# Fused attention and two gated layers: scores of the first batch in one step per buffer, a copy moved to ScalarE, a small sum moved to GpSimd

## The chip, the core and the metric

The kernel runs on one core of a Trainium2 chip. The metric is the time of one execution on the device in microseconds; less is better. The engines named below are TensorE (PE: matmuls, with weight loads PEld beside them), VectorE (DVE), ScalarE (ACT), GpSimd (POOL) and the queue that issues DMAs (SP). Each works through its own queue in the order in which it was written.

## What is computed

Three layers in a row, on a batch of 4 with 576 positions, 8 heads of 64 and 512 channels:

```python
q_rot, k_rot = rotate(q), rotate(k)                  # rotary positions
scores = q_rot @ k_rot.T / 8
attn = exp(scores - max(scores)); attn /= sum(attn) + 1e-9
x = attn @ v                                         # heads side by side: 512 channels
xk, xr = mix of x and x one position earlier
k = relu(xk @ w_k); v = k * k @ w_v
x = sigmoid(xr @ w_r) * v
h = relu(x @ w_in); u, v = halves of h
out = (u * (w_spatial @ normalized(v) + b_spatial)) @ w_out
```

## The kernel before, in words

Attention works in 72 **units**, 18 for each of the 4 batches. A batch has 4 pairs of heads; a pair's 576 query rows make four units of 128 rows and a rest of 64, and the rests of two neighbouring pairs share a unit, the **tail** (units 4 and 13 of a batch). In a common unit the two buffers (`j` = 0 and 1) are the two heads of the pair: head 0 lies in partitions 0 to 63, head 1 in 64 to 127, so their score matmuls use different row groups of TensorE. In a tail the two buffers are the two pairs.

The steps of a unit, by their names in `unit(m)`:

- `scores` (line 338 in the first batch, in plain fp32; lines 327 and 330 later, with split operands): rotated q against rotated k into two score buffers `s` in PSUM, of two banks each, one set for all units. So a unit's scores wait until the exponentials of the unit before have read these buffers.
- `top(j)` (342): VectorE takes the negative maximum of each row of buffer j. `expo(j)` (347): ScalarE's exponential, with the row sums, into `p`.
- `total` (351): the sums plus 1e-9, two numbers per row, on ScalarE. `norm` (354): VectorE's reciprocal. `spread` (358): ScalarE spreads the result over 64 columns.
- `turn(n)`, n = 0, 1, 2 (lines 367 to 381): TensorE turns P through PSUM in three parts; part 0 needs the first exponential, part 1 the second, part 2 holds what is left of P and the spread reciprocals. `take(n)` (395) copies them to `pt`: parts 0 and 1, 128x512, on ScalarE, part 2, 128x256, on VectorE (in a tail each part is two smaller copies).
- After every second common unit (once in nine units, after the tail that follows it) `values` (402) multiplies `pt` by v, twenty matmul records, and `gather` (414) scales the result.

Beside this run the rotation of q and k for later pairs (`prep`, lines 249 to 272, VectorE mostly), the splitting of 16 blocks of the weights `w_k` and `w_v` into a high and a low part (lines 151 to 174, on ScalarE, VectorE and GpSimd), and, from the second batch on, the next layer's matmuls for the batch that is finished (`feed`, lines 498 and 537). During the first batch no such matmuls are there to fill TensorE.

The order of all this is written out before the kernel is built by a planner (`Plan`). Every step is added with an engine, an assumed duration, the steps it needs, and a rank. The planner plays the steps through: at each point it takes, of an engine's steps that are ready within 0.3 us (on TensorE at once), the one of lowest rank, and so it fixes each engine's queue. GpSimd's steps and some of VectorE's are assumed to exclude each other. The assumed durations thus decide places in the queues, while the times on the chip may be others.

Of the kernel before, what the change touches and what calls it, by code (L numbers as in the profile page):

```python
# [7 lines left out]
F32 = mybir.dt.float32  # L8
# [3 lines left out]
AF = mybir.ActivationFunctionType  # L12
ALU = mybir.AluOpType
AX = mybir.AxisListType
PSUM = bass.MemoryType.PSUM
# [10 lines left out]
EXACT = NP  # L26
WB, GB, WB2, GB2 = 3, 2, 3, 2
RAW, ROT, VB, PFB, PTB, XTS = 2, 4, 2, 3, 2, 6
KB, RLB, VSB = 4, 2, 1
EARLY, EVERY = 24, 2.9  # L30
WAIT, SWITCH, BONUS = 0.3, 0.1, 0.0
SIDES = slice(0, HALF), slice(HALF, S)
HEAD = slice(0, 64), slice(64, 128)
# [17 lines left out]
class Plan:  # L51
# [5 lines left out]
    def add(self, eng, us, fn, deps=(), rank=0.0, after=0.12, take=None, give=None, port=False, kind=None):  # L57
        s = Step(eng, us, fn, deps, rank, after, take, give, port, kind)
        self.steps.append(s)
        return s  # L60
# [44 lines left out]
def body(ctx: ExitStack, tc, qp, kp, vp, cs, mu_k, mu_r, w_k, w_v, w_r, w_in, w_sp, b_sp, w_out, out):  # L105
    nc = tc.nc

    const = ctx.enter_context(tc.tile_pool(name="const", bufs=1))
# [6 lines left out]
    ps_m = ph1p.enter_context(tc.tile_pool(name="ps_m", bufs=1, space=PSUM))  # L115
    att = ExitStack()
    at = att.enter_context(tc.tile_pool(name="att", bufs=1, side="right"))
    ps_s = att.enter_context(tc.tile_pool(name="ps_s", bufs=2, space=PSUM, side="right"))
    ps_t = att.enter_context(tc.tile_pool(name="ps_t", bufs=1, space=PSUM, side="right"))
    stage = [at, WB, GB]  # L120

# [5 lines left out]
    ends = [[at.tile([128, 128], F32R, tag=f"qe{i}{k}", name=f"qe{i}{k}") for k in range(2)] for i in range(2)]  # L127
    ident = const.tile([128, 128], F32, name="ident")
    mix4 = const.tile([128, NP, 4], F32, name="mix4")
    epsc = const.tile([128, 3], F32, name="epsc")  # L130
    warm = const.tile([128, 1], F32, name="warm")

    turn_of = {"ww": 0, "wg": 0}
# [72 lines left out]
    add = plan.add  # L206
# [5 lines left out]
    ropes, vloads, exps, turned, valued, xdone, stored = {}, {}, {}, {}, {}, {}, {}  # L212
# [5 lines left out]
    def constants():  # L218
        nc.gpsimd.memset(epsc[:, 0:1], 1e-6)
        nc.gpsimd.memset(epsc[:, 1:2], -0.5)  # L220
        nc.gpsimd.memset(epsc[:, 2:3], 1e-9)
        nc.gpsimd.memset(ident, 0.0)
        for x in ends[0] + ends[1]:
            nc.gpsimd.memset(raw(x), 0.0)
        nc.gpsimd.affine_select(out=ident, in_=ident, compare_op=ALU.not_equal, fill=1.0, base=0,
                                pattern=[[-1, 128]], channel_multiplier=1)
# [76 lines left out]
    units, scored, duos, freed = {}, {}, {}, {}  # L303

    def unit(m):
        w = which(m)
        tail = len(w) == 2
        st = units[m] = {}
# [3 lines left out]
                for n in ((4 * g + 1, 4 * g + 2) if tail else (4 * g + (k - (k > 4)) // 2,))]  # L312
        duo = into[0]

        def scores(halves=(0, 1)):
            if 0 in halves:
                st["s"] = [ps_s.tile([128, 2, 512], F32, tag="s", name=f"s{2 * m + j}") for j in range(2)]
                st["sm"] = at.tile([128, 4, 2], F32, tag="sm", bufs=4, name=f"sm{m}")
            ps = st["s"]
            if w[0][0] >= EXACT:  # L320
                for u, (i, c) in enumerate(w):
                    t = qk[i]
                    for n, (a, b) in enumerate((("hi", "hi"), ("hi", "lo"), ("lo", "hi"))):
                        for h in range(2):
                            x, f = slice(h * HALF, h * HALF + HALF), dict(start=n == 0, stop=n == 2)
                            if tail:
                                nc.tensor.matmul(ps[u][:, h, :HALF], ends[i % 2][a == "lo"], t[b, 1][:, x], **f)  # L327
                            else:
                                for j, r in enumerate(HEAD):
                                    nc.tensor.matmul(ps[j][:, h, :HALF], t[a, 0][r, 128 * c:128 * c + 128], t[b, 1][r, x], **f)  # L330
                return
            for u, (i, c) in enumerate(w):
                q, k = qk[i][0], qk[i][1]
                for h in halves:
                    for j in range(2):
                        r = HEAD[j]
                        o = ps[u][r, h, :HALF] if tail else ps[j][:, h, :HALF]
                        nc.tensor.matmul(o, q[r, 128 * c:min(128 * c + 128, S)], k[r, h * HALF:(h + 1) * HALF],  # L338
                                         start=True, stop=True)

        def top(j):
            nc.vector.tensor_reduce(st["sm"][:, 0, j:j + 1], st["s"][j][:, :, :HALF], axis=AX.XY, op=ALU.max, negate=True)  # L342
# [5 lines left out]
                                 bias=st["sm"][:, 0, j:j + 1], scale=1.0, accum_out=st["sm"][:, 1, j:j + 1])  # L348

        def total():  # L350
            nc.scalar.activation(st["sm"][:, 2, :], st["sm"][:, 1, :], AF.Identity, bias=epsc[:, 2:3])

        def norm():
            nc.vector.reciprocal(st["sm"][:, 3, :], st["sm"][:, 2, :])
# [28 lines left out]
        def take(n, eng):  # L383
            for u, d in enumerate(into):
                if "pt" not in d:
                    d["pt"] = at.tile([128, 10, 320], F32, tag=f"pt{d['n'] % PTB}", name=f"pt{d['n']}")
                o = d["pt"][:, 4 * n:min(4 * n + 4, 10), 256:320]
                if not tail:
                    o, x = d["pt"][:, 4 * n:min(4 * n + 4, 10), 128 * part:128 * part + 128], st["t", n]
                    x = x if n < 2 else x[:, 0:2, :]  # L390
                elif n < 2:
                    x = st["t", n].rearrange("p c (h q) -> p (c h) q", h=2)[:, 4 * u:4 * u + 4, :]
                else:
                    x = st["t", n][:, u, :].rearrange("p (h q) -> p h q", h=2)
                nc.scalar.copy(o, x) if eng == "ACT" else nc.vector.tensor_copy(o, x)  # L395
# [24 lines left out]
        need = [ropes[i] for i, _ in w]  # L420
        if m == 0:
            need = ropes["first"][1] + [add("PE", 0.6, lambda: scores((0,)), ropes["first"][0], -1.0, kind="s")]
        scored[m] = s = add("PE", 0.55 if m == 0 else (2.0 if tail else 1.07) if w[0][0] < EXACT else 1.58 if tail else 0.8, (lambda: scores((1,))) if m == 0 else scores, need + [exps.get((m - 1, j)) for j in range(2)], m - 1.0, kind="s")
        mx = [add("DVE", 0.75, lambda j=j: top(j), [s], m - 0.6) for j in range(2)]
        for j in range(2):
            exps[m, j] = add("ACT", 0.93, lambda j=j: expo(j), [mx[j]] + [turned.get((m - PFB, n)) for n in range(4)],
                             m - 0.5)
        t = add("ACT", 0.2, total, [exps[m, 1]], m - 0.3)
        nm = add("DVE", 0.17, norm, [t], m - 0.3)
        sp = add("ACT", 0.26, spread, [nm], m - 0.3)  # L430
        ready = [[exps[m, 0], exps[m, 1]] if tail else [exps[m, 0]], [exps[m, 1]], [sp]]
        for n in range(3):
            turned[m, n] = add("PE", (0.5, 0.5, 0.8)[n] if tail else (0.44, 0.44, 0.22)[n], lambda slot, n=n: turn(n, slot),
                               ready[n], m + 0.1 * n, take="t", kind="t")
            eng = ("ACT", "ACT", "DVE")[n]
            x = add(eng, ((0.68, 0.68, 0.55) if tail else (0.59, 0.59, 0.42))[n], lambda n=n, eng=eng: take(n, eng),
                    [turned[m, n]] + [y for d in into for y in freed.get(d["n"] - PTB, [])], m - 0.2, give=turned[m, n])
            for d in into:
                d["ev"].append(x)
        if part and k != 3 or tail:  # L440
# [3 lines left out]
            x = add("DVE", 0.49 if duo["cols"] > 256 else 0.42, gather, [v] + mixed.get(i - XTS, []), m + 0.5, give=v)  # L444
# [449 lines left out]
```

## Time and profile before

| what | value |
|---|---|
| median of 3 runs | 777.69 us (777.66 to 781.87) |
| the profiled execution | 777.82 us |
| its span, first to last instruction | 776.0 us |
| TensorE busy (share of the span) | 740.8 us (95%) |
| VectorE | 481.0 us (62%) |
| ScalarE | 463.6 us (60%) |
| GpSimd | 112.2 us (14%) |
| chain that ended last | TensorE 88%, VectorE 4%, ScalarE 3%, DMA 3% |

The profile lists instructions with their start, their duration, and, where an engine stood idle before one, what released it. Busy shares over the whole span mix stages: attention runs to about 450 us, the other layers after it, and the first batch is over at about 102 us. So the rows below are of stretches.

### The profile page before, as it was taken

Reading aid. Unit: us, or ns where it says so; the run is one execution under the profiler, and the core shown is the slowest. Engines: PE = TensorE matmul, PEld = TensorE weight load, DVE = VectorE, ACT = ScalarE, POOL = GpSimd, SP = SyncE. Lnnn points to the kernel's source line nnn. Section 1 sums busy time; section 2 is a strip of 40 time slices with the busy share of each in tenths; the row PEclk is TensorE's granted clock in tenths of the full one; section 3 lists DMA queues with packets and bytes.
Section 4 is the critical chain, followed back from the end, with each engine's and each line's share of the span. In section 5 each row is a group of like instructions: output and inputs, shape, how many; then the busy total and the mean of one; then the engine's idle time right before and its main releaser. Section 6 shows DMA issues by size and latency. Waiting matters only on the chain.

```text
span 776.0 us, 14283 instructions
## 1 busy us (share of the span) xinstructions
PE 740.8 (95%) x5696; PEld 649.9 (84%) x5696; DVE 481.0 (62%) x881; ACT 463.6 (60%) x1061; POOL 112.2 (14%) x132
## 2 busy tenths in 40 slices
PE   4788889999999999999999999999999999999997
PEld 2555569788888888888888898989989999998997
DVE  5988898888777877687856434246463342545111
ACT  3878898778777878778777644245333322533221
POOL 1432424011211211211111000002020000101000
PEclk9999999999999999999999999999999999999999
DMA  8363540542342442533232175072201212010101
GB/s 294 116 201 122 175 129 20 164 149 99 134 163 85 141 156 88 182 113 126 92 131 70 51 268 210 24 264 57 87 1 62 63 46 77 17 31 1 62 1 62
DMA packets 35268, 84.13 MB, mean 108 GB/s; under 512 B 4545, under 2 KB 10433, under 8 KB 35202
## 3 DMA queue, kind: packets, MB, share of 16 engines
q1 hardware_dynamic: 34658, 82.63, 31.6%
q8 instruction: 45, 0.74, 0.4%
q10 hardware_dynamic: 544, 0.59, 0.3%
q14 instruction: 21, 0.17, 0.1%
HBM read 60.65 MB, written 22.55 MB: 107 GB/s over the span
## 4 chain that ended last, share of the span: by engine, by line
PE 88%; DVE 4%; ACT 3%; DMA 3%; issue 0%; SPq 0%; ACTq 0%
PE mv L537 13%; PE mk L498 11%; PE v L402 11%; PE t L378 9%; PE sp L673 8%; PE r L673 7%; PE u L673 7%; PE hv L737 6%; PE o L673 6%; PE s L330 6%; PE s L338 3%; ACT pf L347 1%; DVE raw L249 1%; DMA wi<-wd 1%; PE s L327 1%; DVE sm L342 1%
## 5 line engine op out<-in xcount | busy, mean ns | idle before, releaser
L342 DVE TENSOR_REDUCE sm<-s 128x1 f32<-128x576 f32 x144 | 107.2, 751 | 36.9 <-PE s L330 30.5
L347 ACT ACTIVATE pf<-s,sm 128x576 f32<-128x576 f32 x144 | 107.0, 745 | 14.1 <-DVE sm L342 13.0
L537 PE MATMUL mv<-kh,wv 128*128 128x288 f32 x512 | 114.1, 305 | 1.2 <-ACT kh L512 1.2
L498 PE MATMUL mk<-x,wk 128*128 128x288 f32 x768 | 110.2, 298 | 0.4 <-ACT rl L505 0.4
L395 ACT COPY pt<-t 128x512 f32<-128x512 f32 (+1 forms) x160 | 84.8, 542 | 34.3 <-PE t L378 32.0
L498 PEld LDWEIGHTS mk<-x,wk 128*128 128x128 f32 x768 | 102.9, 188 | 0.7 <-ACT rl L505 0.6
L378 PE MATMUL t<-ident,pf 128*128 128x128 f32 x512 | 82.5, 284 | 14.0 <-ACT pf L347 14.0
L537 PEld LDWEIGHTS mv<-kh,wv 128*128 128x128 f32 x512 | 85.6, 191 | 5.4 <-issue 3.9
L378 PEld LDWEIGHTS t<-ident,pf 128*128 128x128 f32 x512 | 56.6, 141 | 39.9 <-issue 16.4
L402 PE MATMUL v<-pt,vt 128*64 128x256 f32 (+1 forms) x640 | 87.5, 411 | 0.0
L537 PE MATMUL mv<-kl,wv 128*128 128x288 f32 x256 | 76.5, 299 | 0.6 <-DVE kl L516 0.6
L402 PEld LDWEIGHTS v<-pt,vt 128*64 128x64 f32 x640 | 44.3, 136 | 31.7 <-issue 4.1
L673 PE MATMUL sp<-ws,vn 128*128 128x288 f32 x384 | 53.9, 295 | 0.0
L673 PE MATMUL r<-xr,wr 128*128 128x288 f32 x384 | 52.5, 296 | 1.2 <-ACT vs L543 1.2
L673 PE MATMUL o<-g,wo 128*128 128x288 f32 x384 | 52.9, 296 | 0.5 <-ACT os L796 0.5
L673 PEld LDWEIGHTS r<-xr,wr 128*128 128x128 f32 x384 | 51.7, 188 | 1.8 <-ACT vs L543 1.5
L673 PEld LDWEIGHTS sp<-ws,vn 128*128 128x128 f32 x384 | 52.4, 188 | 0.7
L673 PEld LDWEIGHTS o<-g,wo 128*128 128x128 f32 x384 | 51.7, 188 | 1.4 <-ACT os L796 1.2
L673 PE MATMUL u<-x,wi 128*128 128x288 f32 x384 | 52.0, 296 | 0.0
L673 PEld LDWEIGHTS u<-x,wi 128*128 128x128 f32 x384 | 51.6, 188 | 0.3
L537 PEld LDWEIGHTS mv<-kl,wv 128*128 128x128 f32 x256 | 48.9, 191 | 1.2 <-DVE kl L516 1.2
L249 DVE TENSOR_TENSOR raw<-raw,cst 128x1152 f32<-128x1152 f32 (+1 forms) x34 | 45.6, 1344 | 5.7 <-DMA raw<-kp 4.9
(347 smaller groups left out, 1200.3 us busy)
## 6 DMA issues: line engine op xcount, KB each, us to landing
raw<-kp SPq DMA_DIRECT2D x15, 576.0 KB, 3.8
raw<-qp SPq DMA_DIRECT2D x15, 576.0 KB, 4.3
vt<-vp SPq DMA_DIRECT2D x16, 320.0 KB, 3.8
xd<-xt SPq DMA_DIRECT2D x16, 288.5 KB, 3.2
vd<-vs SPq DMA_DIRECT2D x32, 144.0 KB, 1.8
v<-vd SPq DMA_DIRECT2D x16, 288.0 KB, 2.7
out<-os SPq DMA_DIRECT2D x15, 288.0 KB, 2.1
wi<-wd SPq DMA_DIRECT2D x8, 512.0 KB, 9.1
```

Of the source, the lines that this page charges most:

```text
L249: nc.vector.tensor_tensor(t["raw", k][:, :, z], t["raw", k][:, :, z], cst[:, :, z], op=ALU.mult)
L330: nc.tensor.matmul(ps[j][:, h, :HALF], t[a, 0][r, 128 * c:128 * c + 128], t[b, 1][r, x], **f)
L338: nc.tensor.matmul(o, q[r, 128 * c:min(128 * c + 128, S)], k[r, h * HALF:(h + 1) * HALF], start=True, stop=True)
L342: nc.vector.tensor_reduce(st["sm"][:, 0, j:j + 1], st["s"][j][:, :, :HALF], axis=AX.XY, op=ALU.max, negate=True)
L347: nc.scalar.activation(st["p"][:, j, :].rearrange("p (a b) -> p a b", a=2), st["s"][j][:, :, :HALF], AF.Exp, bias=st["sm"][:, 0, j:j + 1], ...
L378: nc.tensor.transpose(pt[:, c, :], p[:, n, k:k + 128], ident)
L395: nc.scalar.copy(o, x) if eng == "ACT" else nc.vector.tensor_copy(o, x)
L402: nc.tensor.matmul(pv[HEAD[j], z], v[:, 4 * j + c if c < 4 else 8 + j, :], pt[:, 4 * j + c if c < 4 else 8, z], start=c == 0, stop=c == 4)
L498: nc.tensor.matmul(ps[:, :HALF], wk[w][:, c, fc * 128:(fc + 1) * 128], a[:, c, :], start=k == 0, stop=k == 11)
L537: nc.tensor.matmul(xs["v", dc][:, :HALF], wv[w][:, fc, dc * 128:(dc + 1) * 128], a, start=k == 0, stop=k == 23)
L673: nc.tensor.matmul(ps[:, h, :HALF], w, a[:, h * HALF:(h + 1) * HALF], start=m == 0, stop=m == n - 1)
L737: nc.tensor.matmul(ps[:, :FS], x[a][:, d, c:c + 128], wi[w][:, d, FS:], start=k == 0, stop=k == 11)
```

## The change

Four things, all for units of the first batch (m < 18):

- `scores` takes a list of buffers. For units 1 to 17 the planner gets two steps, one for each buffer, instead of one for both: step j needs the exponential j of the unit before (not both), the second step needs the first, and `top(j)` needs only step j. In a common unit the matmuls of head 0 are thus written before those of head 1, where before the two heads alternated. The assumed duration is 0.95 us for each step; it was 1.07 us for both (2.0 in a tail). The score buffers get a tag of their own each, with one buffer per tag instead of two buffers of one tag.
- `total` is an addition of two columns on GpSimd, with an assumed 0.37 us, instead of ScalarE's activation. For later units it stays on ScalarE, but its assumed duration is 0.3 instead of 0.2 us. The constants get a fourth column.
- `take(2)` is on ScalarE instead of VectorE, with an assumed 0.38 us (0.55 in a tail).
- Unit 0 keeps its scores in two steps of half the keys each.

```diff
-    ps_s = att.enter_context(tc.tile_pool(name="ps_s", bufs=2, space=PSUM, side="right"))
+    ps_s = att.enter_context(tc.tile_pool(name="ps_s", bufs=1, space=PSUM, side="right"))
...
-        def scores(halves=(0, 1)):
-            if 0 in halves:
-                st["s"] = [ps_s.tile([128, 2, 512], F32, tag="s", name=f"s{2 * m + j}") for j in range(2)]
+        def scores(halves=(0, 1), buffers=(0, 1)):
+            if 0 in halves and 0 in buffers:
+                st["s"] = [ps_s.tile([128, 2, 512], F32, tag=f"s{j}", name=f"s{2 * m + j}") for j in range(2)]
...
                 q, k = qk[i][0], qk[i][1]
+                if tail and u not in buffers:
+                    continue
                 for h in halves:
-                    for j in range(2):
+                    for j in range(2) if tail else buffers:
...
         def total():
-            nc.scalar.activation(st["sm"][:, 2, :], st["sm"][:, 1, :], AF.Identity, bias=epsc[:, 2:3])
+            if m < 18:
+                nc.gpsimd.tensor_tensor(st["sm"][:, 2, :], st["sm"][:, 1, :], epsc[:, 2:4], op=ALU.add)
+            else:
+                nc.scalar.activation(st["sm"][:, 2, :], st["sm"][:, 1, :], AF.Identity, bias=epsc[:, 2:3])
...
-        scored[m] = s = add("PE", 0.55 if m == 0 else (2.0 if tail else 1.07) if w[0][0] < EXACT else 1.58 if tail else 0.8, (lambda: scores((1,))) if m == 0 else scores, need + [exps.get((m - 1, j)) for j in range(2)], m - 1.0, kind="s")
-        mx = [add("DVE", 0.75, lambda j=j: top(j), [s], m - 0.6) for j in range(2)]
+        before = [exps.get((m - 1, j)) for j in range(2)]
+        if 0 < m < APART:
+            sc = [add("PE", 0.95, lambda j=j: scores(buffers=(j,)), need + [before[j]], m - 1.0 + 0.05 * j, kind="s") for j in range(2)]
+            sc[1].deps.append(sc[0])
+        else:
+            sc = [add("PE", 0.55 if m == 0 else (2.0 if tail else 1.07) if w[0][0] < EXACT else 1.58 if tail else 0.8,
+                      (lambda: scores((1,))) if m == 0 else scores, need + before, m - 1.0, kind="s")] * 2
+        scored[m] = sc[1]
+        mx = [add("DVE", 0.75, lambda j=j: top(j), [sc[j]], m - 0.6) for j in range(2)]
...
-        t = add("ACT", 0.2, total, [exps[m, 1]], m - 0.3)
+        t = add(*(("POOL", 0.37) if m < 18 else ("ACT", 0.3)), total, [exps[m, 1]], m - 0.3)
...
-            eng = ("ACT", "ACT", "DVE")[n]
-            x = add(eng, ((0.68, 0.68, 0.55) if tail else (0.59, 0.59, 0.42))[n], lambda n=n, eng=eng: take(n, eng),
+            eng = "ACT" if m < 18 else ("ACT", "ACT", "DVE")[n]
+            x = add(eng, ((0.68, 0.68, 0.55) if tail else (0.59, 0.59, 0.38 if eng == "ACT" else 0.42))[n], lambda n=n, eng=eng: take(n, eng),
```

## Rows read from the trace of the kernel before

**Rows 1.** Busy time by stretch: stretch, its length, PE, PEld, DVE, ACT, POOL (instructions), clock, DMA.

```profile
12.00:102.00 90.00, 73.99 (x528) 46.88 (x528) 79.06 (x145) 74.12 (x184) 32.00 (x26) 1.00 0.48 158
20.00:40.00 20.00, 15.50 (x128) 10.00 (x128) 19.08 (x35) 16.51 (x43) 7.95 (x7) 1.00 0.35 118
140.00:450.00 310.00, 310.00 (x2648) 265.85 (x2647) 231.73 (x434) 237.75 (x594) 46.01 (x42) 1.00 0.36 120
```

**Rows 2.** ScalarE in order of time: start, duration, engine, line, operation, tiles, shape.

```profile
17.06 0.75 ACT L347 ACTIVATE pf<-s,sm 128x576 f32<-128x576 f32 x1
...
62.56 0.59 ACT L395 COPY pt<-t 128x512 f32<-128x512 f32 x1
63.05 0.75 ACT L347 ACTIVATE pf<-s,sm 128x576 f32<-128x576 f32 x1
...
66.65 0.59 ACT L395 COPY pt<-t 128x512 f32<-128x512 f32 x1 [0.32 <-PE t L378]
67.13 0.75 ACT L347 ACTIVATE pf<-s,sm 128x576 f32<-128x576 f32 x1
...
72.52 0.75 ACT L347 ACTIVATE pf<-s,sm 128x576 f32<-128x576 f32 x1
...
102.40 0.75 ACT L347 ACTIVATE pf<-s,sm 128x576 f32<-128x576 f32 x1
```

**Rows 3.** TensorE in order of time, units 9 to 11; the last two: narrower windows.

```profile
60.11 0.66 PE L378 MATMUL t<-ident,pf 128*128 128x128 f32 x4
60.70 1.24 PE L338 MATMUL s<-rot,rot 64*128 64x288 f32 x8
61.87 0.66 PE L378 MATMUL t<-ident,pf 128*128 128x128 f32 x4
...
63.94 0.66 PE L378 MATMUL t<-ident,pf 128*128 128x128 f32 x4 [1.19 <-ACT pf L347]
64.52 1.50 PE L338 MATMUL s<-rot,rot 64*128 64x288 f32 x8
...
66.76 2.90 PE L402 MATMUL v<-pt,vt 128*64 128x256 f32 x20
69.59 0.66 PE L378 MATMUL t<-ident,pf 128*128 128x128 f32 x4
...
61.05 0.65 PE L338 MATMUL s<-rot,rot 64*128 64x288 f32 x4
61.29 0.65 PE L338 MATMUL s<-rot,rot 64*128 64x288 f32 x4
```

**Rows 4.** The chain that ended last: start, duration, what.

```profile
114.16 2.31 PE v L402 x20
```

**Rows 5.** VectorE in order of time, the same units.

```profile
61.97 0.76 DVE L342 TENSOR_REDUCE sm<-s 128x1 f32<-128x576 f32 x1 [0.20 <-PE s L338]
62.78 0.42 DVE L395 COPY pt<-t 128x256 f32<-128x256 f32 x1
63.12 0.75 DVE L342 TENSOR_REDUCE sm<-s 128x1 f32<-128x576 f32 x1
...
65.80 0.76 DVE L342 TENSOR_REDUCE sm<-s 128x1 f32<-128x576 f32 x1 [0.32 <-PE s L338]
```

**Rows 6.** Line 395 by stretch (DVE, ACT); groups by shape: busy us, mean ns.

```profile
12.00:102.00 90.00, 7.30 (x19) 20.51 (x40) 1.00 0.48 158
...
L395 ACT COPY pt<-t 128x256 f32<-128x256 f32 x8 | 2.5, 376 | 0.0
L351 ACT ACTIVATE sm<-sm,epsc 128x2 f32<-128x2 f32 x18 | 5.3, 296 | 0.6
...
L744 POOL TENSOR_TENSOR st<-st,epsc 128x1 f32<-128x1 f32 x18 | 5.6, 316 | 200.1 <-DVE st L743 200.1
```

**Rows 7.** TensorE in order of time at the end of a tail's first part.

```profile
34.35 0.51 PE L338 MATMUL s<-rot,rot 64*128 64x288 f32 x1
34.41 0.22 PE L367 MATMUL t<-ident,pf 64*128 64x64 f32 x1
34.47 1.19 PE L338 MATMUL s<-rot,rot 64*128 64x288 f32 x7
```

More of the change, by code (lines that the diff above doesn't have):

```diff
@@ L30 @@
 EARLY, EVERY = 24, 2.9
+APART = 18
 WAIT, SWITCH, BONUS = 0.3, 0.1, 0.0
@@ L129, in body @@
     mix4 = const.tile([128, NP, 4], F32, name="mix4")
-    epsc = const.tile([128, 3], F32, name="epsc")
+    epsc = const.tile([128, 4], F32, name="epsc")
     warm = const.tile([128, 1], F32, name="warm")
@@ L220, in constants @@
         nc.gpsimd.memset(epsc[:, 1:2], -0.5)
-        nc.gpsimd.memset(epsc[:, 2:3], 1e-9)
+        nc.gpsimd.memset(epsc[:, 2:4], 1e-9)
         nc.gpsimd.memset(ident, 0.0)
```

## Prediction

> **What bounds the kernel now.** I read the busy time by stretch first. In the long middle, 140 to 450 us, TensorE is busy 310.00 of 310 us: that stretch costs what its matmuls cost, and no step of the other engines' queues shortens it [rows 1]. The first batch, 12 to 102 us, is different: TensorE 73.99 of 90 us, VectorE 79.06, ScalarE 74.12, GpSimd 32.00. No engine is full there, so it is waits that are to be looked for, and what is saved in it moves the start of the full stretch and so the end.
>
> The next view is ScalarE in order of time. The first exponential of unit 1 starts at 17.06 us, that of unit 18 at 102.40: 85.34 us for 17 units, 5.02 us each [rows 2]. From unit 10 (63.05) to unit 12 (72.52) two units take 9.47 us; this pair recurs, tails apart, and I work with it.
>
> In the same pair TensorE runs: turning of the last unit's first part (60.11), scores (60.70), turning of the other parts (61.87), then a wait; again first part (63.94), scores (64.52), other parts, values (66.76), up to the next first part at 69.59 [rows 3]. Three waits lie in these 9.48 us. (1) 1.19 us before 63.94, for the exponential. (2) 0.26 us inside the second scores block, 1.50 against 1.24 us: its second buffer was still being read. (3) 0.59 us inside the values, 2.90 against 2.31 us of the same twenty matmuls where nothing is late [rows 3, 4]: they wait for ScalarE's copy of the second part, which ends at 66.65 + 0.59 = 67.24, after they began at 66.76 [rows 2, 3]. Sum 2.04 us in 9.48; over 17 units, 8.5 pairs, 17.3 us.
>
> What ends last in wait 1? The maximum of the first buffer is done at 61.97 + 0.76 = 62.73, but its exponential starts at 63.05, because ScalarE first does the copy of 62.56 that stands ahead of it in its queue [rows 2, 5]. In the next unit the maximum is done at 65.80 + 0.76 = 66.56 and the exponential starts at 67.13, behind the copy of 66.65: 0.57 us late. And the second maximum stands behind VectorE's copy of the last part: 61.97 to 63.12 is 1.15 us for a 0.76 us instruction.
>
> **The change part by part.**
> *VectorE's copies go.* Between 12 and 102 us that is 19 copies, 7.30 us of the 79.06 [rows 6]; the next instruction starts 0.34 us after such a copy (62.78 to 63.12 [rows 5]), so the queue gets 19 x 0.34, some 6 us, back. What is late next is the second exponential, which then waits for the first one (745 ns) and not for VectorE.
>
> *ScalarE gets them and loses the sum.* A 128x256 copy on ScalarE shows 376 ns in the tail units [rows 6]; between nothing and the 0.59 us of a 128x512 copy [rows 2] I take that for all 20 pieces (16 units with one, two tails with two smaller ones). 20 x 0.376 = 7.5 us in, 18 x 0.296 = 5.3 us out [rows 6]: ScalarE rises by 2.2 us to some 76 of 90. It hides as long as ScalarE has those idle 14 us; without that cover it would be 2.2 us. Behind the moved copy wait the next exponentials and the values, which need it last of their five steps, some 1.8 us after they start.
>
> *GpSimd gets the sum.* Its queue holds the weights' additions, 26 instructions in 32.00 us, 1.2 us each [rows 1]. A tiny addition there takes 316 ns [rows 6], about the 296 ns that ScalarE took, so the chain sum, reciprocal, spread, third part only gains a hop. Busy 36% of the time, GpSimd makes a sum wait half an instruction, 0.6 us, in one unit of three, or longer where the addition ahead itself waits; VectorE's reciprocal waits with it, and the maxima behind that in VectorE's queue. Bounds: 0, if the planner's place for it fits, to 18 x 0.36 x 0.6 = 4 us. I take 0.5 us: the reciprocal has time, since the third part is turned after the second. The memset of one more column is nothing: it runs before the first scores.
>
> *Scores in two steps.* One block now alternates the two heads (row groups), eight matmul records in 1.17 us to the next start (60.70 to 61.87). In two steps all four records of one head come before those of the other. The price per unit: 0, if the second head's records overtake and run beside the first's; four pair steps more, 4 x 0.24 = 0.96 us, if they queue (pairs start at 61.05 and 61.29 [rows 3]); a second block's 1.17 us if work is put between the two. The row nearest to this: a record of the next scores starts at 34.35, before the last turning record of the step ahead of it in the queue, at 34.41 [rows 7]. Matmuls of one row group do start ahead of older ones of the other. So I take 0.1 us per unit, 15 units (the two tails already went buffer by buffer, unit 0 keeps its own two steps): 1.5 us, lying in wait 1. For this the Trainium skill has a contrary rule ("TensorE: Matmul & The Clock Gate", Part 3): matmuls start and end strictly in program order, only weight loads are pulled ahead. By it the two heads would queue, and this step of the sum would be 15 x 0.96 us instead of 1.5; the row at 34.35 disagrees. The chance for it stands with the rivals.
>
> *What the two steps give.* The first buffer's scores need only the first exponential. Placed by that, their maximum, and then the exponential, is due sooner in the written-out order, and stands ahead of the copy of the second part instead of behind it. That is worth 0.32 us in the one unit and 0.57 in the other, 0.89 us per pair at most; the values then get their copy later, so wait 3 is not won but moved, unless the next scores are put before them. Of wait 2 nothing is gained as long as the first part's turning (0.59 us) fills it. I take a bit over half of 0.89, 0.5 us per pair, plus 0.2 for the second maximum no longer behind a copy: 0.7 x 8.5 = 6.0 us.
>
> *The written-out order after unit 18.* The planner's cost of the sum on ScalarE goes from 0.2 to 0.3, so later steps may change places. I cost this at nothing: TensorE's full queue hides it [rows 1]; if it opened gaps, each would cost its own length.
>
> Sum: -6.0 + 0.5 + 1.5 = -4.0 us. The profiled execution took 777.82 us around a span of 776.0; the median of the runs is 777.69, 0.13 less. **773.8 us** on the profiled one, so 773.7 as a median.
>
> **The rivals.**
> *Packed queues (faster).* If the two buffers decouple wholly, the fullest engine sets the pace. ScalarE then has 76 us of work where it needs 90, VectorE 72. VectorE reaches 19.08 of 20 us today where it is fullest [rows 1], 95%; ScalarE at 95% needs 80 us: 10 us less, 768. For it: all three waits are of order, not of work. Against: TensorE's values (2.3 us or more) still stand between scores in one queue, and 95% on every engine is rare.
>
> *Unpaired scores (slower).* If the second head's records do queue behind the first's, TensorE gets 15 x 0.96 = 14.4 us. Wait 1, 1.19 x 8.5 = 10.1 us, can take that up; the other 4.3 us lengthen the batch: 782. If the planner also puts other work between the steps, 15 x 1.17 - 10.1 = 7.4 us, 785. It decides from 10.1 / 15 = 0.67 us more per unit. For it: the alternation of heads is what keeps a block at 1.17 us. Against: the overtaking record [rows 7]. The rule of the Trainium skill named above is this rival's.
>
> *It doesn't do what it says (no change).* The first part's turning and the first scores step come due together, after the same exponential. If the turning stays ahead, the first scores start where they do now, 0.59 us after it; the written-out order shifts little, GpSimd's late sums take back 2 to 4 us, and the time is 776 to 779, taken at 777.5.
>
> **How the numbers follow.** Chances: forecast 0.42 (own range 770 to 776), packed 0.17, unpaired 0.18, no change 0.23. The range takes the forecast's range, the no-change case, most of packed from 768.5 and the unpaired one to 782: 768.5 to 782, leaving out under 2 in 10 (half of packed, the spread steps, late sums on top). 1% is 7.8 us, about what a measurement of this kernel can tell from no change. Faster than 769.9 happens in packed and a few of the forecast's: 0.17. Slower than 785.5 needs the spread, unpaired case and late sums: 0.06. Within: 0.77.
>
> **What would show it.** Right: the first exponential of unit 18 some 4 us earlier than 102.40; ScalarE's exponential next to its maximum's end, before the copy of the second part; the wait before the turning well below 1.19 us; VectorE's busy time between 12 and 102 us about 7 us lower; two scores steps together not over 1.3 us plus the wait for the second exponential. Wrong: scores of one unit at 1.9 us or more, idle time on VectorE before the reciprocal with GpSimd named, or gaps on TensorE after 140 us.

## The result and the profile after

The changed kernel takes 787.15 us (787.08 to 788.51), the kernel before 778.5 beside it: ratio 1.0107, 95% interval [1.0074, 1.014], so 8.7 us slower, where 4 us less was forecast. The profiled execution took 787.08 us around a span of 785.3, 9.3 more than the span before.

Busy time by stretch of the changed kernel (columns as in [rows 1]; the third line is cut at other places):

```profile
12.00:102.00 90.00, 88.18 (x484) 54.07 (x486) 64.59 (x113) 65.56 (x167) 31.93 (x39) 1.00 0.45 146
140.00:450.00 310.00, 307.62 (x2625) 262.57 (x2624) 235.51 (x443) 240.70 (x603) 52.16 (x49) 1.00 0.37 121
...
102.00:200.00 98.00, 92.99 (x781) 79.92 (x779) 86.56 (x149) 78.31 (x195) 26.67 (x23) 1.00 0.35 112
```

Against [rows 1], VectorE fell by 14.47 us between 12 and 102 us, ScalarE by 8.56, and TensorE rose by 14.19 to 88.18 of 90: it is the bound now. This stretch holds less of the changed kernel's first batch, which ends later; counted from 12 us to each kernel's first exponential of unit 18 (108.20 us, before 102.40), TensorE's busy time rose from 74.39 to 94.14 us, by 19.8. What ran on it is in the costliest groups between 12 and 102 us, first of the kernel after, then of the one before (busy us, mean ns | idle time before, by what):

```profile
L341 PE MATMUL s<-rot,rot 64*128 64x288 f32 (+1 forms) x152 | 46.7, 472 | 0.1
L384 PE MATMUL t<-ident,pf 128*128 128x128 f32 x116 | 20.6, 310 | 3.2 <-ACT pf L350 3.2
```

```profile
L338 PE MATMUL s<-rot,rot 64*128 64x288 f32 (+1 forms) x152 | 25.8, 440 | 0.0
L378 PE MATMUL t<-ident,pf 128*128 128x128 f32 x128 | 21.6, 292 | 12.8 <-ACT pf L347 12.8
```

The same 152 score records take 20.9 us more. The wait for the exponential, 12.8 us before, is down to 3.2: it was won, and filled with scores. TensorE in order of time shows why, in the units of [rows 3]:

```profile
61.35 1.24 PE L341 MATMUL s<-rot,rot 64*128 64x288 f32 x4
62.52 0.66 PE L384 MATMUL t<-ident,pf 128*128 128x128 f32 x4
63.10 1.23 PE L341 MATMUL s<-rot,rot 64*128 64x288 f32 x4
64.27 0.66 PE L384 MATMUL t<-ident,pf 128*128 128x128 f32 x4
...
65.07 1.23 PE L341 MATMUL s<-rot,rot 64*128 64x288 f32 x4
66.24 2.38 PE L408 MATMUL v<-pt,vt 128*64 128x256 f32 x20
```

Between the two steps of a unit the planner puts turning or values. A block of four records of one head then takes 1.17 us to the next start (61.35 to 62.52), as eight of both heads did (60.70 to 61.87 [rows 3]).

ScalarE's exponentials in order of time say where the time is lost (units 5, 18 and 71 of after; then units 5 and 71 of before, whose unit 18 is in [rows 2]):

```profile
43.61 0.75 ACT L350 ACTIVATE pf<-s,sm 128x576 f32<-128x576 f32 x1
...
108.20 0.75 ACT L350 ACTIVATE pf<-s,sm 128x576 f32<-128x576 f32 x1
...
450.81 0.75 ACT L350 ACTIVATE pf<-s,sm 128x576 f32<-128x576 f32 x1
```

```profile
36.88 0.76 ACT L347 ACTIVATE pf<-s,sm 128x576 f32<-128x576 f32 x1
...
440.55 0.75 ACT L347 ACTIVATE pf<-s,sm 128x576 f32<-128x576 f32 x1
```

Up to unit 5, 6.7 us are lost. From there to unit 18, 0.9 are won (64.59 us, before 65.52), though all common units in it run unpaired. From unit 18 to unit 71, 4.5 are lost (342.61, before 338.15), and the end gives 1.0 back (334.5 against 335.5; the profiled execution of before had a stretch at half pace there, 470.1 to 473.5). Together 9.3, the difference of the spans.

**The first loss is at half pace.** TensorE at the start, after, then before:

```profile
13.21 2.29 PE L341 MATMUL s<-rot,rot 64*128 64x288 f32 x4
...
29.71 2.28 PE L341 MATMUL s<-rot,rot 64*128 64x288 f32 x4
31.92 4.16 PE L408 MATMUL v<-pt,vt 128*64 128x256 f32 x20
36.01 0.66 PE L384 MATMUL t<-ident,pf 128*128 128x128 f32 x4
```

```profile
13.50 2.29 PE L338 MATMUL s<-rot,rot 64*128 64x288 f32 x8
15.73 0.81 PE L378 MATMUL t<-ident,pf 128*128 128x128 f32 x4
...
25.34 1.24 PE L338 MATMUL s<-rot,rot 64*128 64x288 f32 x8
```

The same instruction takes twice as long until about 35.6 us after, until 16.1 before: the lower of TensorE's two levels, 1.2 and 2.4 GHz. (The clock column writes 1.00 for a stretch ahead of the first recorded change; there the durations tell.) At half pace a unit's two unpaired blocks take 2 x 2.2 us, and TensorE is nearly full from 12 to 36 us, and full from then on:

```profile
12.00:36.00 24.00, 22.40 (x68) 13.11 (x68) 13.80 (x22) 12.72 (x31) 9.27 (x10) 1.00 0.50 167
36.00:102.00 66.00, 65.78 (x418) 40.96 (x418) 50.78 (x91) 52.83 (x136) 22.66 (x29) 1.00 0.43 139
```

**The second loss is mostly idle time after unit 18.** TensorE's waits from 102 to 200 us (us in total, times, longest), after and before:

```profile
PE t L384 <- ACT pf L350: 4.0, 2, 2.3
```

```profile
PE t L378 <- ACT pf L347: 1.2, 1, 1.2
```

Counted from unit 18 to unit 71, TensorE stands idle for 4.77 us, before for 1.67, and its 2886 records keep it busy for 337.84 us, before for 336.48: of the 4.5 us 3.1 are idle time. With the waits goes a late first matmul on the last split weight, the value weights w_v (after, then before):

```profile
154.35 0.40 PE L550 MATMUL mv<-kh,wv 128*128 128x288 f32 x1
```

```profile
139.44 0.38 PE L537 MATMUL mv<-kh,wv 128*128 128x288 f32 x1
```

### The profile page after: what moved, and what is told of

Its sections match the earlier page's. It is cut to its first block, busy times and chain, and to the rows that moved or that the text cites. A ratio compares the mean times of both kernels' runs of the same rounds, so it can differ in the third digit from the quotient of the medians.

```text
span 785.3 us, 14264 instructions
## 1 busy us (share of the span) xinstructions
PE 760.8 (97%) x5696; PEld 661.5 (84%) x5696; DVE 473.8 (60%) x861; ACT 461.8 (59%) x1063; POOL 115.5 (15%) x150
## 4 chain that ended last, share of the span: by engine, by line
PE 91%; DVE 4%; DMA 3%; ACT 2%; issue 1%; SPq 0%; ACTq 0%; DVEq 0%
PE mv L550 12%; PE v L408 11%; PE mk L511 10%; PE t L384 8%; PE sp L686 8%; PE r L686 7%; PE u L686 7%; PE hv L750 6%; PE o L686 6%; PE s L331 6%; PE s L341 6%; PE s L328 1%; DMA wi<-wd 1%; PE t L386 1%; PE t L387 1%; DMA wr<-wd 1%
## 5 line engine op out<-in xcount | busy, mean ns | idle before, releaser
L401 ACT COPY pt<-t 128x512 f32<-128x512 f32 (+1 forms) x180 | 90.4, 523 | 55.1 <-PE t L384 46.2
L350 ACT ACTIVATE pf<-s,sm 128x576 f32<-128x576 f32 x144 | 107.0, 745 | 13.1 <-DVE sm L345 11.9
L550 PE MATMUL mv<-kh,wv 128*128 128x288 f32 x512 | 110.6, 301 | 1.2 <-ACT kh L525 1.2
L550 PEld LDWEIGHTS mv<-kh,wv 128*128 128x128 f32 x512 | 84.0, 188 | 3.9 <-issue 2.4
L408 PEld LDWEIGHTS v<-pt,vt 128*64 128x64 f32 x640 | 46.2, 139 | 32.7 <-issue 7.1
L341 PE MATMUL s<-rot,rot 64*128 64x288 f32 (+1 forms) x160 | 49.2, 487 | 8.0 <-DVE rot L258 7.9
```

The lines of the kernel that those rows point to most:

```text
L350: nc.scalar.activation(st["p"][:, j, :].rearrange("p (a b) -> p a b", a=2), st["s"][j][:, :, :HALF], AF.Exp, bias=st["sm"][:, 0, j:j + 1], ...
L408: nc.tensor.matmul(pv[HEAD[j], z], v[:, 4 * j + c if c < 4 else 8 + j, :], pt[:, 4 * j + c if c < 4 else 8, z], start=c == 0, stop=c == 4)
L550: nc.tensor.matmul(xs["v", dc][:, :HALF], wv[w][:, fc, dc * 128:(dc + 1) * 128], a, start=k == 0, stop=k == 23)
```

## The experiments

Theory: the split does it. Its halves are put apart, cost a whole block each, and cost most at half pace; the rest follows in the order. Rivals: the sum's hop over GpSimd; one-head matmuls slow wherever they stand; half pace by itself; the weights late. Times are medians, ratios against the kernel before in the same job, with 95% intervals.

### One part alone

```diff
# copies_only: the kernel before with
-            eng = ("ACT", "ACT", "DVE")[n]
+            eng = "ACT" if m < 18 else ("ACT", "ACT", "DVE")[n]
...
# sum_only: the kernel before with
-        t = add("ACT", 0.2, total, [exps[m, 1]], m - 0.3)
+        t = add(*(("POOL", 0.37) if m < 18 else ("ACT", 0.2)), total, [exps[m, 1]], m - 0.3)
...
# split_only: the kernel before with scores(buffers=(j,)) in two steps
# no_split: the changed kernel with
-APART = 18
+APART = 1
```

> The kernel before with the third part's copy of units 0 to 17 on ScalarE and nothing else of the change. Theory S (sum): this part is harmless or helps, 774 to 779, unit 18 not later than 103 us, TensorE at full pace from about 16 us on. Theory K (copies): ScalarE's longer queue delays exponentials, 781 to 785, with falls of the pace in the first batch.

> The kernel before with the sum of units 0 to 17 on GpSimd and nothing else of the change. With one scores step per unit but copies and sum moved, the time was still 6 per mille over the kernel before, with a VectorE reciprocal late (82.56 us, 4 us after its sum), TensorE waiting 2.1 us for the third part, and half pace after it. Theory S (sum): the step on GpSimd brings this, since the written-out order puts reciprocals later: unit 18 at 105 to 110 us, 781 to 785. Theory K (copies): the copies bring it: 777 to 779 here.

> The kernel before with the split scores of units 1 to 17 and nothing else of the change. Theory A (pace): half pace until about 35 us again, units 4 and 5 some 6 us late, little lost from there to unit 18; 782 to 787 with what the order after unit 18 does. Theory B (work): full pace at about 16 us, losses spread evenly over the units, 1 us each. If the split is harmless by itself: 777 to 779.

> The changed kernel with one scores step per unit as before; the copies on ScalarE and the sum on GpSimd stay. Theory A and B both: unit 18 starts at 100 to 103 us, as before or a little earlier. Theory C (order): TensorE's idle time between 100 and 200 us, 5.0 us changed against 1.7 us before, comes from the order after the first batch and not from the split, so it stays: 778 to 781. If the split alone brought it: 775 to 778.

Measured: copies alone 779.24 us, 0.9994 [0.9974, 1.0015]; the sum alone 785.03, 1.0065 [1.004, 1.0091]; the split alone 792.19, 1.0153 [1.01, 1.0205]; copies and sum without the split 784.13, 1.006 [1.0038, 1.0081]. The busy time from 12 to 102 us, copies alone and split alone:

```profile
12.00:102.00 90.00, 74.17 (x510) 47.58 (x510) 76.59 (x131) 77.41 (x200) 35.22 (x29) 0.98 0.50 165
```

```profile
12.00:102.00 90.00, 88.28 (x492) 54.05 (x492) 66.90 (x126) 66.59 (x167) 24.06 (x21) 1.00 0.43 141
```

The split fills TensorE by itself (88.28; its profiled execution took 787.50 us), and its loss is larger than any expectation named. The copies gain nothing, though they give VectorE time. The sum loses too. The parts don't add: by their ratios 11.9 us for the split (7.8 to 16.0) and 5.1 for the sum alone, 8.3 for the whole change.

Units 18 and 71 of no_split miss what was expected of them, and they limit what the first loss can be put down to:

```profile
110.70 0.75 ACT L350 ACTIVATE pf<-s,sm 128x576 f32<-128x576 f32 x1
...
447.57 0.75 ACT L350 ACTIVATE pf<-s,sm 128x576 f32<-128x576 f32 x1
```

Without the split, unit 18 comes even later than in the changed kernel, by 2.5 us, and from there to unit 71 it takes 336.9 us, 5.7 less. So a late unit 18 is not the split's alone; the longer stretch behind it is what the split adds to the other two parts.

### Pairs kept together

late_split splits from unit 6 on only. glued has the planner place the second scores step directly behind the first. With that, the assumed durations (0.6 and 0.85 us in a common unit instead of 0.95 each) and the rank of these steps change too, so the order shifts in other places as well. glued_no_sum leaves the sum on ScalarE besides. heads_in_turn is the kernel before with all of head 0's matmuls ahead of head 1's in its one step.

```diff
# late_split
-        if 0 < m < APART:
+        if 5 < m < APART:
# glued, in the planner: the step named by then follows at once
+            if s.then is not None:
+                x = s.then
+                x.begin = max([free[s.eng]] + [d.end + d.after for d in x.deps])
+                free[s.eng] = x.end = x.begin + x.us
+                ...
# and in unit(), where Begun is met once the exponential has begun
...
+            sc[0].deps.append(Begun(before[1]))
+            sc[0].then = sc[1]
# heads_in_turn
-                for h in halves:
-                    for j in range(2):
+                for h, j in [(h, j) for h in halves for j in range(2)] if tail else [(h, j) for j in range(2) for h in halves]:
```

> The kernel before, with nothing changed but the order of a unit's four score matmuls: both of head 0, then both of head 1, in one step. If matmuls of different row groups run beside each other even when they are not written alternately (overtaking): the block of eight records stays at 1.2 to 1.5 us and the time at 777 to 779. If they queue in program order: the block takes 2.1 to 2.2 us, TensorE gets 0.96 us in each of 15 units, and the time is 780 to 783 or, if the pace comes late too, more.

> The changed kernel with the split scores for units 6 to 17 only (units 1 to 5 as before). Theory A (pace): units 1 to 5 pair again, TensorE reaches full pace at about 16 us, and nearly all of the 6.7 us comes back: 780 to 781, with unit 18 no later than 103 us. Theory B (work): three common units pair again, 3 x 1.17 = 3.5 us back: 783 to 784.

> The changed kernel with the second scores step of a unit always put directly behind the first in TensorE's order (units 1 to 17), so that nothing stands between the two buffers; copies on ScalarE and the sum on GpSimd stay. Separation theory (what is lost in the first 45 us is the work put between the two halves of a pair, and the half pace that goes with it): half pace ends near 16 us instead of 35.6, unit 5's first exponential is near 37 us instead of 43.6, some 6 us come back and what is left is the sum's part: 779 to 784. Row-group theory (eight scores in a row of one row group each are slow in themselves, wherever they stand): the pace and unit 5 stay as in the changed kernel, 785 to 788.

> As the one before, but the small sum stays on ScalarE. If separation and the sum together are the whole loss: 776 to 779, no worse than the kernel before. If something else of the split (the order after unit 18, the late weight splitting) holds by itself: 782 or more, with unit 18's first exponential already at or under 102.4 us.

heads_in_turn: 778.85 us, 1.001 [0.9998, 1.0023]. Its block takes 1.18 us to the next start, no longer than in turns:

```profile
61.22 1.25 PE L337 MATMUL s<-rot,rot 64*128 64x288 f32 x8
62.40 0.66 PE L377 MATMUL t<-ident,pf 128*128 128x128 f32 x4
```

So the order of heads costs nothing as long as the two stand together. late_split: 787.76 us, 1.0108 [1.0083, 1.0133]; unit 5 comes at 37.34 us and not 43.61, but unit 18 at 108.58 (half pace came back three times, 13.7 us in sum). glued: 781.33 us, 1.0026 [1.0006, 1.0046], 6 of the 8.7 us back, with the scores in the split's two steps and its buffers:

```profile
62.76 2.38 PE L424 MATMUL v<-pt,vt 128*64 128x256 f32 x20
65.06 1.25 PE L357 MATMUL s<-rot,rot 64*128 64x288 f32 x8
66.24 0.66 PE L400 MATMUL t<-ident,pf 128*128 128x128 f32 x4
```

Eight records in 1.18 us again: it is the work between, not the two steps. Half pace went at 16.3 us as expected but was back from 19.7 to 30.0, so unit 5 came at 39.70, not 37.

```profile
107.19 0.75 ACT L366 ACTIVATE pf<-s,sm 128x576 f32<-128x576 f32 x1
```

The 338.4 us from unit 18 to unit 71 are as before the change: the second loss is gone. But unit 18 comes only 1.0 us earlier than in the changed kernel, 4.8 later than in the kernel before: most of the first loss stays. glued_no_sum: 783.68 us, 1.006 [1.0036, 1.0084], unit 18 at 105.23. It fits neither expectation: without the sum it is no faster than glued, so no run shows that the sum is what glued still loses.

### Pace

12 small matmuls ahead of the first scores and, in the runs with a 2, 8 behind them, into a buffer that nobody reads. after_heat, after_heat2: on the changed kernel; before_heat2: on the one before.

```diff
+    def heat(n):
+        ps = ps_m.tile([128, 512], F32, tag="m0", name="heat")
+        for _ in range(n):
+            nc.tensor.matmul(ps[:, :128], ident, ident, start=True, stop=True)
+    add("PE", 4.0, lambda: heat(12), [first], -20)
...
+        if m == 0:
+            add("PE", 1.0, lambda: heat(8), [scored[0]], -0.9)
```

> The changed kernel plus twelve 128x128 fp32 matmuls of the identity with itself on TensorE, before the first scores, into a PSUM buffer that nothing reads. Theory A (pace): with the scores split TensorE stays at half pace until 36.18 us, where the kernel before left it at about 16.2 us, and that costs the 6.7 us by which units 4 and 5 are late; with the extra matmuls full pace comes by about 12 us and the time falls by 6 to 8 us, to 779 to 781. Theory B (work): the split gives TensorE 1.17 us more in each of 15 units, at any pace; the extra matmuls lie in time in which TensorE idles, and the time stays at 786 to 787.

> The kernel before plus matmuls of the identity with itself that nothing reads: twelve before the first scores, eight right behind unit 0's scores. With the first twelve alone (on the changed kernel) full pace came at 7.6 us and was lost at 11.0 us, when TensorE had waited for the first exponential. If the second eight hold it, unit 1's scores run at full pace (1.24 us instead of 2.29) and unit 1's exponential starts 1 to 2 us earlier than 17.06: 775.5 to 777, faster than the kernel before. If the pace is lost all the same: 777.5 to 779.

> The changed kernel with 12 small matmuls ahead of the first scores and 8 behind them that write a buffer nobody reads, so that TensorE reaches full pace early and does not stand still between units 0 and 1. If the half pace to 35.6 us is the cause of the first 6.7 us: full pace holds from about 8 us on, unit 5's first exponential comes near 37 to 38 us and the time is 780 to 783. If eight matmuls of one row group take as long as 16 paired ones at either pace and that alone is the cause: unit 5 stays past 41 us and the time 785 to 788. If half pace comes back while units 1 to 5 run, the run tells nothing of the first.

after_heat: 787.74 us, 1.012 [1.0102, 1.0137]; full pace came at 7.6 us, was lost at 11.0 and back only at 34.9, so it tells nothing of the pace. before_heat2: 779.18 us, 0.9992 [0.9972, 1.0012]: full pace from 8.1 us on brings unit 18 to 100.81, 1.6 us earlier, and no measurable time. after_heat2: 785.39 us, 1.0093 [1.0072, 1.0114]. It runs the changed kernel's order with full pace from 12.7 to 22.9 us, then half pace to 33.2:

```profile
13.00:22.80 9.80, 7.73 (x39) 4.87 (x38) 7.52 (x10) 7.30 (x16) 4.91 (x4) 1.00 0.62 209
23.00:33.00 10.00, 10.00 (x34) 5.42 (x34) 5.31 (x11) 4.76 (x12) 4.70 (x6) 0.50 0.51 172
```

Here both paces stand beside each other. The first exponentials of units 1 and 2, of after_heat2 and then of the changed kernel:

```profile
16.45 0.75 ACT L350 ACTIVATE pf<-s,sm 128x576 f32<-128x576 f32 x1
...
22.01 0.74 ACT L350 ACTIVATE pf<-s,sm 128x576 f32<-128x576 f32 x1 [0.58 <-DVE sm L345]
```

```profile
17.26 0.74 ACT L350 ACTIVATE pf<-s,sm 128x576 f32<-128x576 f32 x1
...
24.94 0.75 ACT L350 ACTIVATE pf<-s,sm 128x576 f32<-128x576 f32 x1
```

From unit 1 to unit 2 it takes 5.56 us, the changed kernel at half pace 7.68, the kernel before 5.23: half pace is 2.1 us of that unit's loss. What is left for the separation at full pace, 0.3, is no more than this unit varies without it (5.97 us in before_heat2, 14.76 to 20.73). In the second stretch TensorE is full at half pace and the loss is back. Unit 5 comes 2.69 us earlier than in the changed kernel, unit 18 2.68. So half pace is 2.7 us of the 6.7 by this run; more can't be had from it, as the pace did not hold.

### The sum and the exclusion of the port

The planner lets a step on GpSimd exclude certain VectorE steps, on a port that it takes the two engines to share. These kernels take the exclusion from the sum's step, and change nothing of the instructions: sum_free is sum_only, after_free the changed kernel, glued_free glued, no_split_free no_split, each with

```diff
         t = add(*(("POOL", 0.37) if m < 18 else ("ACT", 0.3)), total, [exps[m, 1]], m - 0.3)
+        t.port = False
```

> The kernel before with the small sum on GpSimd, as in the run of the sum alone (785.0), but the planner is told that this sum doesn't exclude VectorE's steps that share the port with GpSimd, so that it doesn't shift them. If the order that the planner makes of the exclusion is what costs: 777 to 780. If it is GpSimd's own time on the way from exponential to reciprocal: 783 to 786 again.

> The changed kernel with the planner told that the sum on GpSimd doesn't exclude VectorE's steps on the shared port, and nothing else. If the sum's part adds to the split's: 782 to 784 (4 of the 5 us that this brought in the kernel with the sum alone). If TensorE, which is busy 98% of the time between 12 and 102 us here, hides it: 786 to 788.

> The glued kernel (second scores step directly behind the first) with the same for the planner's exclusion. If what the glued kernel still loses (2 us) is the sum's order: 776 to 779, level with the kernel before or under it. If the rest comes from elsewhere: 780 to 783.

> The changed kernel without the split (copies on ScalarE, sum on GpSimd) with the planner told that this sum doesn't exclude VectorE's steps on the shared port. With the exclusion it took 784.1. If the exclusion is the sum's price: 777 to 780. If the sum on GpSimd costs otherwise: 783 to 785.

sum_free 780.15 us, 1.0015 [0.9995, 1.0035], as the exclusion theory had it. But after_free 794.16, 1.0215 [1.0186, 1.0244], glued_free 783.57, 1.007 [1.0043, 1.0098], no_split_free 783.95, 1.0071 [1.0043, 1.0099]: against the kernels with the exclusion worse, worse and level. The theory holds for the sum alone and falls for the others. One input of the planner that moves no instruction to another engine shifts the time by -4 to +8 us (ratios, each against its kernel without it), by the order that comes out. In the changed kernel GpSimd's sum is waited for once; VectorE's waits there, 12 to 102 us:

```profile
DVE sm L345 <- PE s L341: 19.7, 23, 2.4
DVE xt L420 <- PE v L408: 4.4, 3, 1.7
DVE sm L360 <- POOL sm L355: 0.6, 1, 0.6
```

### The late weights

```diff
# the rank of each block's splitting, in all three
-1.8 * c if k else 17 + 0.7 * (c - 8)
# weights_early: the changed kernel, all blocks
+1.5 * c if k else 11 + 0.7 * (c - 8)
# wv_early: the changed kernel, w_v alone
+1.8 * c if k else 15 + 0.6 * (c - 8)
# weights_late: the kernel before, w_v alone
+1.8 * c if k else 19 + 0.8 * (c - 8)
```

> The changed kernel with the splitting of the weight blocks given earlier ranks, so that its casts lie earlier among the first units. If the 4 us that are lost behind unit 18 come from the late weights (TensorE idle 5.0 us between 100 and 200 us, before 1.7): the idle time falls to 2 to 3 us and the time to 783 to 785. If the late weights only go along with a loss that is elsewhere: 786 to 789.

> The changed kernel with earlier ranks for the splitting of w_v alone, so that its last cast lies by unit 23 (as in the kernel before) and not 25; the first units keep their order. If the late weights cost the 4.4 us behind unit 18: from unit 18 to unit 71 338 to 340 us instead of 342.6, and 782 to 784 in all. If not: 342 to 343 there and 786 to 788.

> The kernel before with later ranks for the splitting of w_v alone: its last cast by unit 27 instead of 23. If late weights cost by themselves: from unit 18 to unit 71 342 us or more instead of 338.2, and 782 or more in all. If they are only a mark of something else: 338 to 339 there and 777 to 780.

weights_early: 803.58 us, 1.033 [1.0305, 1.0354]: the splitting crowds the first units (unit 18 at 123.70), it tells nothing of the weights. weights_late: 783.39 us, 1.0066 [1.0049, 1.0082]. Unit 18 (102.62) is as before, the first matmul on w_v comes at 160.67 against 139.44, and unit 71 5.5 us later (a stretch at half pace, 142.2 to 145.6, is part of it); TensorE waits from 102 to 200 us much as in the changed kernel:

```profile
102.62 0.74 ACT L347 ACTIVATE pf<-s,sm 128x576 f32<-128x576 f32 x1
...
446.03 0.75 ACT L347 ACTIVATE pf<-s,sm 128x576 f32<-128x576 f32 x1
```

```profile
PE t L378 <- ACT pf L347: 3.2, 2, 2.0
```

Later ranks for w_v thus cost 5.1 us by themselves, with nothing changed up to unit 18; how much of it is the lateness and how much the order that comes with it, this run doesn't tell. wv_early: 787.38 us, 1.0122 [1.0101, 1.0142], unit 18 to unit 71 341.7 us: brought forward in the changed kernel they cost as much. From unit 24 on 2.1 us come back (301.5 us to unit 71, after 303.6), but units 18 to 24 take 1.2 more (40.3, after 39.1) and unit 18 comes 0.5 later. That there is no free place for them once TensorE is full is a guess from this. So is the idea that the second loss follows from the fuller TensorE of the first batch. It doesn't follow from a late unit 18: no_split has that, and no second loss.

**All orders together.** No version beat the kernel before. The scatter of orders is a rival to every single comparison above, so it helps to line them all up. The eight kernels with the two steps apart lie at 1.0093 to 1.033 of the kernel before, the eleven others at 0.9992 to 1.0071: every order with the pair apart was slower than every order with it together, though the nearest two intervals overlap (after_heat2 and no_split_free). Unit 18 does not tell the two groups apart: it starts between 105.5 and 109.0 us in the first (weights_early left out), between 100.8 and 111.3 in the second. The stretch from unit 18 to unit 71 nearly does: 341.7 to 345.4 us, with 339.9 for late_split, against 336.9 to 341.0, with 343.4 for weights_late.

## Why the prediction was wrong

**Wrong: the scores in two steps.** This step was priced at 0.1 us per unit, 1.5 in all, for two steps that stand together. That price holds where they do (heads_in_turn, glued: 1.18 us per pair). The rule that matmuls start and end strictly in program order, from the Trainium skill ("TensorE: Matmul & The Clock Gate", Part 3), is contradicted by the same 1.18 us, and so is, for such a pair, the sentence at the start that each engine works through its queue in order. Standing together is not enough if the second buffer is still being read. In unit 2 of after_heat2 the two steps follow each other at full pace and take 2.2 us, as the second starts at 18.98, just after ScalarE's second exponential of the unit before (18.09 to 18.83) and the reading of its row sums (to 18.93):

```profile
17.93 2.29 PE L341 MATMUL s<-rot,rot 64*128 64x288 f32 x8
20.15 0.66 PE L384 MATMUL t<-ident,pf 128*128 128x128 f32 x4
```

But the planner puts work between them in nearly every unit, and then the bound that the step itself named, a second block's 1.17 us, is what the rows show. The prediction's own sign of being wrong, scores of one unit at 1.9 us or more, came (two blocks of 1.17). I took the value from a row on overtaking; whether the two would stand together is a question to the planner. Its answer could be read from what the prediction assumed elsewhere: that the first scores come due before the second exponential, with turning due in between.

**Wrong: what the two steps give, 6.0 us.** The wait for the exponential did fall, from 12.8 to 3.2 us, but scores took its place. Nor does ScalarE start the exponential next to its maximum: the maximum of 62.65 ends at 63.39, the exponential starts at 63.89, still behind a copy and a spread.

```profile
62.65 0.74 DVE L345 TENSOR_REDUCE sm<-s 128x1 f32<-128x576 f32 x1
```

```profile
63.21 0.58 ACT L401 COPY pt<-t 128x512 f32<-128x512 f32 x1 [1.11 <-PE t L384]
63.69 0.30 ACT L364 COPY rb<-sm 128x128 f32<-128x128 f32 x1
63.89 0.74 ACT L350 ACTIVATE pf<-s,sm 128x576 f32<-128x576 f32 x1
```

**Nearest: the second half of the unpaired rival**, 785 with work between the steps. TensorE's rise between 12 and 102 us, 14.19, is close to what it worked out for queued pairs (14.4) by chance: over the whole first batch it is 19.8, half pace included. And the loss arose elsewhere than it said. It spread 7.4 us over the batch; from unit 5 to unit 18 the idle time took up the whole rise. It used full-pace prices for the first units, which run at half pace, where a unit's blocks take twice that and hardly any idle time is left (1.6 of 24 us): 6.7 us there. How much of these the separation brings and how much the order and its late pace stays open: no_split_free loses 4.3 us up to unit 5 as well (41.21), without the split.

**Wrong: the order after unit 18 at nothing.** It was looked at for the sum's planned cost alone. The split also fills TensorE in the plan, the weight blocks land later, and TensorE loses 3.3 us of busy time between 102 and 200 us (92.99, before 96.33). The prediction had said that such gaps would cost their own length; from unit 18 to unit 71 they are 3.1 us of the 4.5 lost. The chain from the fuller plan to the late weights is argued, not shown.

**The copies** were a part of those 6.0 us. Alone they raise ScalarE by 3.3 us (77.41, before 74.12; the sum stays there), relieve VectorE by 2.5 (76.59, before 79.06) and bring no time (0.9994). **The sum on GpSimd, 0.5 us (bound 4):** alone 5.1 us (3.1 to 7.1), so near the bound or over it, and 1.2 (-0.4 to 2.7) without the planner's exclusion (sum_free): what the step left out is the order, not the hop. In the changed kernel no run shows a loss by it, and one wait of 0.6 us names it.

## What to carry to other kernels

Before a step is cut in two, ask what the scheduler will put between the halves: a pair that shares an engine by row groups is one step for a reason, and the price of a half is the price of the whole. Price the units at the start from rows at the start, at the pace they run there. Where an order is planned, a forecast below the scatter of plans (here -4 to +8 us for one input that moves no work) is a guess, and single parts can't be added up.

## What was not expected

Half pace in the first batch goes along with what all these kernels lose there. Time at half pace before the first exponential of unit 18, and that exponential, in us, from the clock's recorded changes (before the first of them, half pace), of twelve kernels:

```
kernel          half pace   unit 18      kernel          half pace   unit 18
before_heat2       8.1      100.81       late_split        29.7      108.58
before            16.1      102.40       split_only        33.0      108.99
after_heat2       19.5      105.52       no_split          33.4      110.70
copies_only       25.4      105.05       after             35.6      108.20
sum_free          25.9      105.29       no_split_free     36.0      111.31
glued             28.7      107.19       sum_only          40.5      110.12
```

Over 19 of the 20 profiled kernels (weights_early left out) the correlation is 0.95, with 0.33 us per us. Cause and effect can go both ways: half pace delays, and it can follow a standstill (in after_heat2 TensorE waits 2.09 us up to 22.89, and half pace begins at 22.9). The one direction that was set from outside is the heat: 8.0 us less of it in the kernel before gives 1.6 us, 16.1 less in the changed one 2.7. In the changed kernel TensorE was busy without a break from 12.2 to 24.4 us, all of it at half pace, which lasted to 35.6; in the kernel before it was busy without a break from 12.5 us, and the pace rose at 16.1. How busy TensorE was does not tell the two apart; why full pace stayed away with unpaired scores is open.
